# Reordering the tail of an attention and selected-row feed-forward kernel: row choice, picks, down projection and copies

## The chip, the cores and the metric

The kernel runs on one core of one Trainium2 chip. The metric is device microseconds of one execution. Where a ratio is quoted, it is the mean time of one kernel's fast runs over that of the other's fast runs of the same rounds, so not quite the ratio of the medians given beside it; in the experiments the first run of each kernel is left out of the ratio.

## The reference, cut to what matters

```python
def _A_ref(x, wq, wk, wv, wo):            # 16 query heads, one key/value head
    q = (x @ wq).reshape(B, S, 16, 28).transpose(0, 2, 1, 3)
    k, v = x @ wk, x @ wv
    p = softmax(einsum("bhqd,bkd->bhqk", q, k) * 28 ** -0.5)
    return heads_joined(einsum("bhqk,bkd->bhqd", p, v)) @ wo

def _B_ref(x, w_r, w_gate, w_up, w_down):  # 8 selected rows go through a feed-forward
    r = x @ w_r
    idx = argsort(-r)[:, :8]
    x_sel = x[idx]
    y = (silu(x_sel @ w_gate) * (x_sel @ w_up)) @ w_down
    return x + scatter_add(zeros, idx, y * sigmoid(r[idx]))

h  = x + _A_ref(layernorm(x), ...)         # x is 1 x 2048 x 448
h2 = h + _B_ref(layernorm(h), ...)         # gate/up 448 x 1792, down 1792 x 448
```

## The kernel before

The kernel handles 16 blocks of 128 rows. For each block TensorE forms scores, ScalarE takes most exponentials (VectorE and GpSimd make the rest with integer additions on the bit patterns, stored in Y), TensorE multiplies by the values, and the block's output is projected, added to x and normalized. When the last block is done, the eight rows with the largest router scores are found, gathered, sent through the feed-forward, and written over eight rows of the output. What follows the last exponential is called the tail here.

The program does not write its instructions in order. It declares operations with an assumed duration, what they read and write, and a priority; a planner puts them on the engines' queues. With `port=True` an operation is marked as one that VectorE is not to run beside GpSimd's marked work, and the planner starts it only when GpSimd's planned work with the mark is over:

```python
def dve_choice(self, lst, t, port):
    eff = [(max(o.ready, port) if o.port else o.ready, o) for o in lst]
    ...
```

GpSimd's large additions, its On products (attention output times reciprocal row sums), VectorE's On products of block 15 and others carry the mark. VectorE's On products of block 14 do not. A large addition reads:

```python
G.op(PO, lambda e: e.tensor_tensor(y[3].bitcast(I32), y[0].bitcast(I32),
                                   step3[:, 0:1].broadcast_to([128, 1024]), ALU.add), 2050, reads=r + ["step3"],
     writes=[("Y", n, 3, k) for k in range(4)], prio=t - 20, deps=done, port=True)
```

A check of the row sums reduces minima and maxima and adds the violation counts, one number per partition:

```python
spans = [(lall, lk, LO, HI, ())]          # blocks 0 to 14 together
if not exact:
    spans.append((Rb[:, rb, :], ..., (picked,)))
...
G.op(DV, lambda e: e.tensor_tensor(bad1[:, :], Lmm[:, 2:3], Lmm[:, 3:4], ALU.add), 70,
     reads=[("Ln", 0, 0), ("Ln", 0, 1)], writes=["bad1"])
for k in range(2 if not exact else 0):
    G.op(DV, lambda e, k=k: e.tensor_tensor(bad1[:, :], bad1[:, :], Lmm[:, 6 + k:7 + k], ALU.add), 70,
         reads=["bad1", ("Ln", 1, k)], writes=["bad1"])
```

The end of the kernel: VectorE copies the down projection's result and casts the output rows; then four row writes go out on SyncE's queue and four on ScalarE's. Each queue waits for all 16 ordinary output writes first, since a row write goes over what they wrote:

```python
for h, c in enumerate(halves):
    G.op(PE, mm(ps[0:8, obank[h], 0:224], pick8, part[:, c], False, True), 390, mode="F", ...)
    G.op(DV, lambda e, h=h, c=c: e.tensor_copy(rows8[:, c], ps[0:8, obank[h], 0:224]), 300, ...)
for j in range(8):
    q, ld = (SP, loads[0]) if j < 4 else (AC, loads[1])
    o = G.op(q, lambda e, j=j: e.dma_start(out[0, bass.ds(row[j], 1), :], rows8[j:j + 1, :]), 60,
             reads=[("rows8", 0), ("rows8", 1)] + [("out", k) for k in range(NT)], writes=[("scatter", j)], dma=True)
```

## Time and profile before

| Quantity | us |
|---|---|
| time, median of 3 runs | 389.06 |
| span in the profile | 386.9 |
| ScalarE idle ahead of its last five exponentials, at 361 | 0.76 |
| last exponential ends | 367.80 |
| output-row casts end | 383.29 |
| last exponential to end of casts | 15.49 |
| end of casts to end of span | 3.6 |

In the timeline each row has the start, the length, the engine, source line, operation and tiles, and in brackets the idle time before it with what ended it. Two rows of the timeline of before give the root of the 0.76 us: the residual addition of block 14 (hbuf) and the score matmuls that waited for it.

```profile
360.21 0.61 DVE L771 TENSOR_TENSOR hbuf<-ps,xx 128x448 f32<-128x448 f32 x1
...
360.96 0.40 PE L501 MATMUL ps<-Q,K 32*128 32x512 bf16 x4 [0.69 <-DVE hbuf L771]
```

### The profile page before, as it was taken

Reading aid. Unit: us, or ns where it says so; the run is one execution under the profiler, and the core shown is the slowest. Engines: PE = TensorE matmul, PEld = TensorE weight load, DVE = VectorE, ACT = ScalarE, POOL = GpSimd, SP = SyncE. Lnnn points to the kernel's source line nnn. Section 1 sums busy time; section 2 is a strip of 40 time slices with the busy share of each in tenths; the row PEclk is TensorE's granted clock in tenths of the full one; section 3 lists DMA queues with packets and bytes.
Section 4 is the critical chain, followed back from the end, with each engine's and each line's share of the span. In section 5 each row is a group of like instructions: output and inputs, shape, how many; then the busy total and the mean of one; then the engine's idle time right before and its main releaser. Section 6 shows DMA issues by size and latency. Waiting matters only on the chain.

```text
span 386.9 us, 8691 instructions
## 1 busy us (share of the span) xinstructions
PE 317.0 (82%) x3520; PEld 109.7 (28%) x3523; DVE 336.0 (87%) x706; ACT 365.2 (94%) x308; POOL 192.9 (50%) x185
## 2 busy tenths in 40 slices
PE   7899888878788887878788878878788888788895
PEld 3454332223223222323222222323232222222242
DVE  7996787989899897989798897979898998979973
ACT  4799999999999999999999999999999999999951
POOL 6520134645646375636546365746556464655410
PEclk9999999999999999999999999999999999999999
DMA  7995000010101010010102010010102010110100
GB/s 204 236 228 115 12 9 23 4 64 4 64 3 58 10 38 28 6 62 5 64 3 65 2 45 22 15 54 3 65 2 65 3 52 15 28 40 3 48 27 19
DMA packets 19557, 17.56 MB, mean 45 GB/s; under 512 B 5996, under 2 KB 16764, under 8 KB 19512
## 3 DMA queue, kind: packets, MB, share of 16 engines
q1 hardware_dynamic: 19472, 16.93, 16.2%
q8 instruction: 29, 0.48, 0.5%
q14 instruction: 16, 0.13, 0.1%
q0 software_dynamic: 32, 0.01, 0.0%
q10 hardware_dynamic: 8, 0.00, 0.0%
HBM read 11.43 MB, written 5.52 MB: 44 GB/s over the span
## 4 chain that ended last, share of the span: by engine, by line
ACT 81%; DVE 9%; PE 6%; DMA 1%; SPq 1%; issue 1%; POOL 0%; DVEq 0%
ACT P L928 81%; PE ps L501 5%; DVE bn L650 2%; DMA xx<-in_A_x_dram 1%; DVE Y L1005 1%; DVE xnT L694 1%; SPq L527 1%; DVE xx L679 1%; DVE K L711 1%; DVE mv L652 0%; POOL st L779 0%; DVE On L757 0%; DVE Y L1014 0%; PE ps L504 0%; DVE junk L807 0%
## 5 line engine op out<-in xcount | busy, mean ns | idle before, releaser
L928 ACT ACTIVATE P<-ps 128x1536 bf16<-128x1536 f32 (+1 forms) x281 | 354.2, 1510 | 3.4 <-PE ps L501 3.1
L1005 DVE TENSOR_SCALAR Y<-ps 128x512 int16<-128x512 f32 x240 | 164.9, 687 | 34.1 <-PE ps L501 34.1
L1021 POOL TENSOR_TENSOR Y<-Y,step 128x1024 int32<-128x1024 int32 x59 | 111.6, 1891 | 141.2 <-DVE Y L1014 140.6
L501 PE MATMUL ps<-Q,K 32*128 32x512 bf16 x1024 | 110.6, 382 | 60.7 <-DVE Y L1005 40.2
L501 PE MATMUL ps<-Y,Vs 128*32 128x512 bf16 x960 | 88.7, 384 | 1.6
L501 PEld LDWEIGHTS ps<-Q,K 32*128 32x128 bf16 x1024 | 33.1, 90 | 175.8 <-ACT P L928 168.4
L1014 DVE TENSOR_SCALAR Y<-Y 128x2048 int16<-128x2048 int16 x120 | 81.2, 687 | 0.6
L501 PE MATMUL ps<-P,Vs 128*32 128x512 bf16 x784 | 72.5, 385 | 0.0
L501 PE MATMUL ps<-zero 128*32 128x512 bf16 (+3 forms) x154 | 47.7, 383 | 1.6 <-DVE zero L520 1.2
L501 PEld LDWEIGHTS ps<-Y,Vs 128*32 128x32 bf16 x960 | 23.2, 94 | 31.7 <-issue 14.3
L501 PEld LDWEIGHTS ps<-P,Vs 128*32 128x32 bf16 x784 | 18.8, 94 | 28.1 <-issue 26.1
L754 POOL TENSOR_TENSOR On<-Ot,Rb 128x256 bf16<-128x256 f32 x28 | 19.7, 726 | 12.0 <-DMA Rb<-l_scr 12.0
L779 POOL TENSOR_TENSOR st<-st,nhalf 128x1 f32<-128x1 f32 x15 | 18.4, 1226 | 6.7 <-DVE st L777 6.7
L501 PEld LDWEIGHTS ps<-zero 128*32 128x32 bf16 (+1 forms) x157 | 13.5, 99 | 14.2 <-issue 6.8
L501 PE MATMUL ps<-xnT,wq_pad 112*128 112x128 bf16 x256 | 17.4, 220 | 0.0
L799 POOL TENSOR_SCALAR xx<-hbuf,st 128x448 bf16<-128x448 f32 x15 | 16.2, 1077 | 0.0
L501 PEld LDWEIGHTS ps<-xnT,wq_pad 112*128 112x128 bf16 x256 | 14.4, 98 | 3.6 <-issue 3.4
L501 PE MATMUL ps<-wo_pad,On 128*128 128x448 bf16 x64 | 14.9, 355 | 0.4 <-DVE On L757 0.4
L771 DVE TENSOR_TENSOR hbuf<-ps,xx 128x448 f32<-128x448 f32 x15 | 9.4, 623 | 2.3 <-PE ps L501 2.3
L637 DVE TENSOR_SCALAR Q<-ps,qone 128x512 bf16<-128x512 f32 x15 | 11.2, 749 | 0.0
L796 POOL TENSOR_SCALAR xx<-hbuf,st 128x448 bf16<-128x448 f32 x15 | 10.9, 726 | 0.5 <-DVE st L793 0.5
L650 DVE BATCH_NORM_STATS2 bn<-xx 128x6 f32<-128x448 bf16 x16 | 9.8, 613 | 1.2 <-DMA xx<-in_A_x_dram 1.1
(198 smaller groups left out, 172.5 us busy)
## 6 DMA issues: line engine op xcount, KB each, us to landing
Rb<-l_scr SPq DMA_DIRECT2D x14, 256.0 KB
x_scr<-xx SPq DMA_DIRECT2D x15, 224.0 KB, 2.4
out_dram<-xx SPq DMA_DIRECT2D x16, 112.0 KB, 1.7
wg_sb<-in_B_w_gate_dram SPq DMA_DIRECT2D x1, 1568.0 KB, 14.8
wu_sb<-in_B_w_up_dram SPq DMA_DIRECT2D x1, 1568.0 KB, 20.9
wd_sb<-in_B_w_down_dram SPq DMA_DIRECT2D x1, 1568.0 KB, 26.3
xx<-in_A_x_dram SPq DMA_DIRECT2D x3, 448.0 KB, 6.0
wq_sb<-in_A_wq_dram SPq DMA_DIRECT2D x2, 196.0 KB, 2.9
```

The source lines that it names most:

```text
L501: return lambda e: e.matmul(o, lhsT=l, rhs=r, start=start, stop=stop)
L637: G.op(DV, lambda e: e.tensor_scalar(Q[:, q, :, :].rearrange("p g n -> p (g n)"), ps[:, bank, :], qone[:, 0:1], None, ALU.add), dvt(512), ...
L650: G.op(DV, lambda e, t=t: e.bn_stats(bn6[:, t, :], x_sb[:, t, :]), dvt(D), reads=[("x", t)], writes=[("bn6", t)])
L754: G.op(PO, lambda e, c=c: e.tensor_tensor(On[:, rb, c], Ot[:, rb, c], Rb[:, rb, c], ALU.mult), 750, reads=[both[h], rk[h]], writes=[("On", ...
L771: G.op(DV, lambda e: e.tensor_tensor(hbuf[:, hr, :], ps[:, bank, 0:D], x_sb[:, t, :], ALU.add), dvt(D), reads=[pk(bank), ("x", t)], writes ...
L779: G.op(PO, lambda e: e.tensor_tensor(st[:, t, 4:5], st[:, t, 7:8], nhalf[:, 0:1], ALU.pow), 600, reads=[("st7", t), "nhalf"], writes=[("st ...
L796: G.op(PO, lambda e: e.tensor_scalar(outf[:, t, :], hbuf[:, hr, :], st[:, t, 5:6], st[:, t, 6:7], ALU.mult, ALU.add), 800, reads=[("h", hr ...
L799: G.op(PO, lambda e: e.tensor_scalar(xn[:, t, :], hbuf[:, hr, :], st[:, t, 4:5], st[:, t, 6:7], ALU.mult, ALU.add), 800, reads=[("h", hr), ...
L928: acts.append(G.op(AC, lambda e: e.activation(P[:, s0:s0 + w, :], ps[:, b0:b0 + w, :], ACT.Exp, bias=-(ZERO + SHIFT) * OCT, scale=OCT), w ...
L1005: G.op(DV, lambda e: e.tensor_scalar(Y[:, y, 0, q, :].bitcast(I16), ps[:, vb, :], 0.0, 32639.0 - STEP[3], ALU.max, ALU.min), dvt(512), rea ...
L1014: done = [G.op(DV, lambda e, c=c: e.tensor_single_scalar(y[c].bitcast(I16), y[0].bitcast(I16), STEP[c], ALU.add), 600, reads=r, writes=[(" ...
L1021: G.op(PO, lambda e: e.tensor_tensor(y[3].bitcast(I32), y[0].bitcast(I32), step3[:, 0:1].broadcast_to([128, 1024]), ALU.add), 2050, reads= ...
```

## The change

The intent is to shorten the chain of the tail, step by step, and to close the hole ahead of the last five exponentials. The core of the diff, with cuts marked:

```diff
-HINT = {PE: 118, AC: 8, DV: 8, PO: 1, SP: 6}
+HINT = {PE: 118, AC: 8, DV: 8, PO: 3, SP: 6}
...                                        (On products of the last blocks)
-                     reads=[both[h], rk[h]], writes=[("On", rb, h)], prio=G.prio - 500)
+                     reads=[both[h], rk[h]], writes=[("On", rb, h)], prio=G.prio - 500, urgent=not exact, port=True)
...                                        (GpSimd's large addition, third batch of block 15, is deferred)
+        if b == NB - 1 and j == 2:
+            done += [G.last_w[("On", b % 2 ^ 1, h)][-1] for h in range(2)] + [G.last_w[("st2", b - 2)][-1]]
...                                        (row choice alone; score broadcast later)
-        G.op(PE, [mm(ps[:, SB[1], 8:16], oneF[:, :], top8[:, :], True, True),
-                  mm(ps[0:8, SB[1], 24:25], eq8[0:NC1, :], cidx[:, :], True, True)], 400, mode="F", ...
+        G.op(PE, mm(ps[0:8, SB[1], 24:25], eq8[0:NC1, :], cidx[:, :], True, True), 200, mode="F", ..., prio=hot - 70)
...
+        G.op(PE, mm(ps[:, SB[1], 8:16], oneF[:, :], top8[:, :], True, True), 250, mode="F", ..., prio=hot + 9)
...                                        (picks: row numbers early, scores behind the up projection)
+    G.op(PE, [mm(ps[:, xbank, 0:1], rep4(128, 0), rsig[:, 1:2], True, False),
+              mm(ps[:, xbank, 0:1], rep4(8, 1), cols[:, 1:2], False, True)], 600, mode="F", deps=risen[-1:], ...
...                                        (down projection in two column halves, in two banks)
-            G.op(PE, [mm(ps[32 * c:32 * c + 32, dbank, 0:D], guT[0:CK, k, 32 * c:32 * c + 32], wd_sb[0:CK, 4 * c + k, :],
-                         k == 0, k == 3) for c in range(4)], 189, mode="V", ...
+        for n, x in enumerate(halves):
+            for k in (2 * h, 2 * h + 1):
+                down = G.op(PE, [mm(ps[32 * c:32 * c + 32, dbank[n], 0:224], guT[0:CK, k, 32 * c:32 * c + 32],
+                                    wd_sb[0:CK, 4 * c + k, x], k == 0, k == 3) for c in range(4)], 105, mode="V", ...
...                                        (copies and casts: one half on VectorE, one on ScalarE)
+    o = G.op(AC, lambda e: e.activation(part[:, halves[1]], ps[:, dbank[1], 0:224], ACT.Identity), 350, ...
...
+    G.op(DV, lambda e: e.tensor_copy(rows8[:, halves[0]], rest(0)), 300, ...
+    o = G.op(AC, lambda e: e.activation(rows8[:, halves[1]], rest(1), ACT.Identity), 350, ...
...                                        (row-sum check in three parts instead of two)
+        spans.append((Lc[:, NB - 2, :], [("Lc", NB - 2)], LO, HI, ()))
...
-    for k in range(2 if not exact else 0):
-        G.op(DV, lambda e, k=k: e.tensor_tensor(bad1[:, :], bad1[:, :], Lmm[:, 6 + k:7 + k], ALU.add), 70, ...
+    for n, k in ((n, k) for n in range(1, len(spans)) for k in range(2)):
+        G.op(DV, lambda e, n=n, k=k: e.tensor_tensor(bad1[:, :], bad1[:, :], Lmm[:, 4 * n + 2 + k:4 * n + 3 + k], ALU.add),
+             70, reads=["bad1", ("Ln", n, k)], writes=["bad1"])
```

More of the change, by code (lines that the diff above doesn't have):

```diff
@@ L428, in _main @@
     Rc = sb("Rc", [128, 2, 16], F32)
-    Lmm = sb("Lmm", [128, 8], F32)
+    Lmm = sb("Lmm", [128, 12], F32)
     Rb = sb("Rb", [128, 2, 512], F32)
@@ L493, in _main @@
     scr128 = junk[:, 0:128]
+    junk2 = xnT[:, 0, 0:896].bitcast(F32)
     R0, R1, VB, ACC = 5, 6, 6, 7
@@ L781, in out_proj @@
         if hurry:
-            G.op(DV, lambda e: e.scalar_tensor_tensor(junk[:, :], hbuf[:, hr, :], 1.0, w_rb[:, :], ALU.mult, ALU.mult,
+            G.op(DV, lambda e: e.scalar_tensor_tensor(junk2, hbuf[:, hr, :], 1.0, w_rb[:, :], ALU.mult, ALU.mult,
                                                       accum_out=st[:, t, 2:3]), 700,
-                 reads=[("h", hr), "w_rb"], writes=["junk", ("st2", t)], port=True, prio=G.prio - 890, urgent=True)
+                 reads=[("h", hr), "w_rb"], writes=[("xnT", k) for k in range(7)] + [("st2", t)], port=True, prio=G.prio - 890, urgent=True)
             G.op(DV, lambda e: e.tensor_scalar(st[:, t, 3:4], mv[:, t, 0:1], sw[:, 0:1], st[:, t, 2:3],
@@ L961, in sum_group @@
             o = G.op(PE, [None] * len(lst), 216, mode="V", pos=[x[0] for x in lst], reads=reads, deps=snap[1:] + first_sum,
-                     prio=G.prio - 0.005)
+                     prio=G.prio - 1.0)
             o.name = lst
@@ L1070, in stage2 @@
              reads=[pk(SB[1]), "pcol"], writes=["eq8"])
-        G.op(PE, [mm(ps[:, SB[1], 8:16], oneF[:, :], top8[:, :], True, True),
-                  mm(ps[0:8, SB[1], 24:25], eq8[0:NC1, :], cidx[:, :], True, True)], 400, mode="F",
-             reads=["cidx", "eq8", "oneF", "top8"], writes=[pk(SB[1])])
+        G.op(PE, mm(ps[0:8, SB[1], 24:25], eq8[0:NC1, :], cidx[:, :], True, True), 200, mode="F",
+             reads=["cidx", "eq8"], writes=[pk(SB[1])], prio=hot - 70)
         G.op(DV, lambda e: e.tensor_copy(cols[:, 0:1], ps[0:8, SB[1], 24:25]), 130, reads=[pk(SB[1])], writes=["cols0"])
         G.op(DV, lambda e: e.tensor_copy(idxu[:, :], cols[:, 0:1]), 70, reads=["cols0"], writes=["idxu"])
-        G.op(DV, lambda e: e.tensor_copy(bc[:, :], ps[:, SB[1], 8:16]), 130, reads=[pk(SB[1]), "cols0"], writes=["bc"], name="bc")
+        G.op(PE, mm(ps[:, SB[1], 8:16], oneF[:, :], top8[:, :], True, True), 250, mode="F", reads=["oneF", "top8"],
+             writes=[pk(SB[1])], prio=hot + 9)
+        G.op(DV, lambda e: e.tensor_copy(bc[:, :], ps[:, SB[1], 8:16]), 130, reads=[pk(SB[1])], writes=["bc"], name="bc",
+             prio=hot + 9)
     ot, sops, acts = [], [], []
@@ L1199, in _main @@
     G.prio = hot
-    rbank, xbank, gbank, ubank, tbank, kbank, dbank = 0, 1, 3, 6, 4, 4, 1
-    obank = (2, 6)
+    rbank, xbank, gbank, ubank, tbank, kbank, dbank = 0, 1, 3, 6, 4, 4, (1, 3)
+    obank = (2, 0)
     G.op(PE, mm(ps[:, rbank, 0:128], rp[:, t:t + 1].broadcast_to([128, 128]), ident[:, :], True, True), 60, mode="F",
@@ L1227, in _main @@
         for ch in range(NCH)]
-    wide(gbank, wg_sb, "wg_sb")
-    wide(ubank, wu_sb, "wu_sb")
+    halves = (slice(0, 224), slice(224, 448))
+    rest = lambda h: ps[32 * h:32 * h + 8, obank[h], 0:224]
+    for h, c in enumerate(halves):
+        G.op(PE, mm(rest(h), oh[0:8, 1, :], both8[:, c], True, False), 100, mode="F", reads=["oh1", "both8"],
+             writes=[pk(obank[h])], prio=hot + 1)
+    wide(gbank, wg_sb, "wg_sb")
+    risen = wide(ubank, wu_sb, "wu_sb")
+    G.prio = hot + 60
+    G.op(PO, lambda e: e.memset(junk[:, 128:384], 0.0), 300, reads=["junk"], writes=["ohf0", "ohf1"], prio=hot)
+    G.op(DV, lambda e: e.tensor_copy(ohf[:, 0, :, 0:8], oh[:, 0, :].unsqueeze(1).broadcast_to([128, 4, 8])), 90,
+         reads=["oh0"], writes=["ohf0"])
+    G.op(DV, lambda e: e.tensor_copy(ohf[0:8, 1, :, 0:8], oh[0:8, 1, :].unsqueeze(1).broadcast_to([8, 4, 8])), 90,
+         reads=["oh1"], writes=["ohf1"])
+    rep4 = lambda n, a: ohf[0:n, a, :, :].rearrange("p c n -> p (c n)")
+    G.op(PE, [mm(ps[0:1, kbank, 8:16], rsig[:, 0:1], ohf[:, 0, 0, 0:8], True, False),
+              mm(ps[0:1, kbank, 8:16], cols[:, 0:1], ohf[0:8, 1, 0, 0:8], False, True)], 200, mode="F",
+         reads=["ohf0", "ohf1", "rs0", "cols0"], writes=[pk(kbank)], prio=hot + 2)
+    G.op(DV, lambda e: e.tensor_copy(idx2, ps[0:1, kbank, 8:16]), 130, reads=[pk(kbank)], writes=["idx2"])
+    G.op(PE, [mm(ps[:, xbank, 0:1], rep4(128, 0), rsig[:, 1:2], True, False),
+              mm(ps[:, xbank, 0:1], rep4(8, 1), cols[:, 1:2], False, True)], 600, mode="F", deps=risen[-1:],
+         reads=["ohf0", "ohf1", "rs1", "cols1"], writes=[pk(xbank)])
+    G.op(DV, lambda e: e.tensor_scalar(pick8, mask8, ps[:, xbank, 0:1], None, ALU.mult), 90, reads=[pk(xbank), "mask8"],
+         writes=["pick8"])
+    G.prio = hot
     for h in range(2):
@@ L1250, in _main @@
     for h in range(2):
-        for k in (2 * h, 2 * h + 1):
-            G.op(PE, [mm(ps[32 * c:32 * c + 32, dbank, 0:D], guT[0:CK, k, 32 * c:32 * c + 32], wd_sb[0:CK, 4 * c + k, :],
-                         k == 0, k == 3) for c in range(4)], 189, mode="V", reads=[("guT", h), "wd_sb"],
-                 writes=[pk(dbank)])
-    halves = (slice(0, 224), slice(224, 448))
-    for h, c in enumerate(halves):
-        G.op(DV, lambda e, c=c: e.tensor_copy(part[:, c], ps[:, dbank, c]), 300, reads=[pk(dbank)],
-             writes=[("part", h)])
@@ L1259, in _main @@
-    G.prio = hot + 60
-    G.op(PO, lambda e: e.memset(junk[:, 128:384], 0.0), 300, reads=["junk"], writes=["ohf0", "ohf1"], prio=hot)
-    G.op(DV, lambda e: e.tensor_copy(ohf[:, 0, :, 0:8], oh[:, 0, :].unsqueeze(1).broadcast_to([128, 4, 8])), 90,
-         reads=["oh0"], writes=["ohf0"])
-    G.op(DV, lambda e: e.tensor_copy(ohf[0:8, 1, :, 0:8], oh[0:8, 1, :].unsqueeze(1).broadcast_to([8, 4, 8])), 90,
-         reads=["oh1"], writes=["ohf1"])
-    rep4 = lambda n, a: ohf[0:n, a, :, :].rearrange("p c n -> p (c n)")
@@ L1266, in _main @@
-    G.op(PE, [mm(ps[:, rbank, 0:1], rep4(128, 0), rsig[:, 1:2], True, False),
-              mm(ps[:, rbank, 0:1], rep4(8, 1), cols[:, 1:2], False, True),
-              mm(ps[0:1, rbank, 8:16], rsig[:, 0:1], ohf[:, 0, 0, 0:8], True, False),
-              mm(ps[0:1, rbank, 8:16], cols[:, 0:1], ohf[0:8, 1, 0, 0:8], False, True)], 600, mode="F",
-         reads=["ohf0", "ohf1", "rs0", "rs1", "cols0", "cols1"], writes=[pk(rbank)])
-    G.op(DV, lambda e: e.tensor_scalar(pick8, mask8, ps[:, rbank, 0:1], None, ALU.mult), 90, reads=[pk(rbank), "mask8"],
-         writes=["pick8"])
@@ L1273, in _main @@
-    G.op(DV, lambda e: e.tensor_copy(idx2, ps[0:1, rbank, 8:16]), 130, reads=[pk(rbank)], writes=["idx2"])
-    for h, c in enumerate(halves):
-        G.op(PE, [mm(ps[0:8, obank[h], 0:224], oh[:, 0, :], outf[:, t, c], True, False),
-                  mm(ps[0:8, obank[h], 0:224], oh[0:8, 1, :], both8[:, c], False, False)], 200, mode="F",
-             reads=["oh0", "oh1", ("outf", t), "both8"], writes=[pk(obank[h])])
+        for n, x in enumerate(halves):
+            for k in (2 * h, 2 * h + 1):
+                down = G.op(PE, [mm(ps[32 * c:32 * c + 32, dbank[n], 0:224], guT[0:CK, k, 32 * c:32 * c + 32],
+                                    wd_sb[0:CK, 4 * c + k, x], k == 0, k == 3) for c in range(4)], 105, mode="V",
+                            reads=[("guT", h), "wd_sb"], writes=[pk(dbank[n])])
@@ new lines, in _main @@
+    G.op(DV, lambda e: e.tensor_copy(part[:, halves[0]], ps[:, dbank[0], 0:224]), 300, reads=[pk(dbank[0])],
+         writes=[("part", 0)])
+    o = G.op(AC, lambda e: e.activation(part[:, halves[1]], ps[:, dbank[1], 0:224], ACT.Identity), 350,
+             reads=[pk(dbank[1])], writes=[("part", 1)])
+    o.deps[table.idx] = False
+    G.prio = hot + 60
+    for h, c in enumerate(halves):
+        G.op(PE, mm(rest(h), oh[:, 0, :], outf[:, t, c], False, False), 100, mode="F", reads=["oh0", ("outf", t)],
+             writes=[pk(obank[h])], deps=(down,), prio=hot - 1)
@@ L1288, in _main @@
     for h, c in enumerate(halves):
-        G.op(PE, mm(ps[0:8, obank[h], 0:224], pick8, part[:, c], False, True), 390, mode="F",
-             reads=["pick8", ("part", h), pk(obank[h])], writes=[pk(obank[h])])
-        G.op(DV, lambda e, h=h, c=c: e.tensor_copy(rows8[:, c], ps[0:8, obank[h], 0:224]), 300, reads=[pk(obank[h])],
-             writes=[("rows8", h)])
+        G.op(PE, mm(rest(h), pick8, part[:, c], False, True), 390, mode="F", reads=["pick8", ("part", h), pk(obank[h])],
+             writes=[pk(obank[h])])
+    G.op(DV, lambda e: e.tensor_copy(rows8[:, halves[0]], rest(0)), 300, reads=[pk(obank[0])], writes=[("rows8", 0)])
+    o = G.op(AC, lambda e: e.activation(rows8[:, halves[1]], rest(1), ACT.Identity), 350, reads=[pk(obank[1])],
+             writes=[("rows8", 1)])
+    o.deps[table.idx] = False
     done = []
@@ L1301, in _main @@
     G.prio = 7000
-    lall = Lc[:, 0:NB if exact else NB - 1, :].rearrange("p a b -> p (a b)")
-    lk = [("Lc", b) for b in range(NB if exact else NB - 1)]
+    nl = NB if exact else NB - 2
+    lall = Lc[:, 0:nl, :].rearrange("p a b -> p (a b)")
+    lk = [("Lc", b) for b in range(nl)]
     spans = [(lall, lk, LO, HI, ())]
@@ L1311, in _main @@
             G.op(DV, lambda e, m=m, k=k, src=src, red=red: e.tensor_reduce(m[:, k:k + 1], src, AX.X, red),
-                 dvt(512 if n else 256), reads=keys, writes=[("Lm", n, k)], deps=after)
+                 dvt((256, 16, 512)[n]), reads=keys, writes=[("Lm", n, k)], deps=after)
             G.op(DV, lambda e, m=m, k=k, cmp=cmp, lim=lim: e.tensor_single_scalar(m[:, 2 + k:3 + k], m[:, k:k + 1], lim,
@@ L1317, in _main @@
          reads=[("Ln", 0, 0), ("Ln", 0, 1)], writes=["bad1"])
-    for k in range(2 if not exact else 0):
-        G.op(DV, lambda e, k=k: e.tensor_tensor(bad1[:, :], bad1[:, :], Lmm[:, 6 + k:7 + k], ALU.add), 70,
-             reads=["bad1", ("Ln", 1, k)], writes=["bad1"])
-    G.op(PE, mm(ps[0:1, 0, 0:1], bad1[:, :], ones128[:, :], True, True), 100, mode="F", reads=["bad1", "ones128"],
-         writes=[pk(0)])
-    G.op(DV, lambda e: e.tensor_copy(flag[:, :], ps[0:1, 0, 0:1]), 120, reads=[pk(0)], writes=["flag"])
+    for n, k in ((n, k) for n in range(1, len(spans)) for k in range(2)):
+        G.op(DV, lambda e, n=n, k=k: e.tensor_tensor(bad1[:, :], bad1[:, :], Lmm[:, 4 * n + 2 + k:4 * n + 3 + k], ALU.add),
+             70, reads=["bad1", ("Ln", n, k)], writes=["bad1"])
+    G.op(PE, mm(ps[0:1, 6, 0:1], bad1[:, :], ones128[:, :], True, True), 100, mode="F", reads=["bad1", "ones128"],
+         writes=[pk(6)])
+    G.op(DV, lambda e: e.tensor_copy(flag[:, :], ps[0:1, 6, 0:1]), 120, reads=[pk(6)], writes=["flag"])
     G.op(DV, lambda e: e.tensor_copy(bad1[:, :], bad1[:, :]), 70, reads=["bad1", "flag"], writes=["bad1"])
```

## The prediction

> **What bounds the kernel now.** I read the shares of the page first, then the chain that ended last, then the timeline of the last 30 us, and there the stretches in which each engine stood still.
>
> From the page of the kernel before, the shares and the chain:
>
> ```profile
> PE 317.0 (82%) x3520; PEld 109.7 (28%) x3523; DVE 336.0 (87%) x706; ACT 365.2 (94%) x308; POOL 192.9 (50%) x185
> ...
> ACT 81%; DVE 9%; PE 6%; DMA 1%; SPq 1%; issue 1%; POOL 0%; DVEq 0%
> ```
>
> ScalarE's exponentials (281 instructions) are the bound for 81% of the chain, and the change does not touch them up to block 14 of 16. So most of the 386.9 us span cannot move. What can move lies after some 355 us: the last exponential ends at 367.80 (a run of five from 361.41, 6.39 long), and the span goes on for another 19.1 us. In the table by stages ScalarE has no work at all from 380.5 on, and TensorE does in sequence what VectorE hands it. There the bound is the length of a chain, not an engine.
>
> The ScalarE rows of the timeline from 359 to 361.5, and the TensorE rows from 369.9 to 374.1:
>
> ```profile
> 357.52 3.13 ACT L928 ACTIVATE P<-ps 128x1536 bf16<-128x1536 f32 x2
> 361.41 1.45 ACT L928 ACTIVATE P<-ps 128x1536 bf16<-128x1536 f32 x1 [0.76 <-PE ps L501]
> ```
>
> ```profile
> 370.42 0.38 PE L501 MATMUL ps<-top,oneF 1*128 1x8 f32 x2
> 370.73 0.20 PE L501 MATMUL ps<-cidx,eq 120*8 120x1 f32 x2
> 370.86 0.23 PE L501 MATMUL ps<-zero 128*128 128x128 bf16 x1
> 370.92 0.92 PE L501 MATMUL ps<-wo_pad,On 128*128 128x448 bf16 x4
> ```
>
> The first shows the one hole in ScalarE's late stream: 0.76 us at 361. The timeline names its root, since the score matmuls before it waited 0.69 us for the residual addition of block 14, which held their bank. The second shows the score broadcast (top) and the row choice (cidx, eq) ahead of the last output projection.
>
> The timeline around the selected rows:
>
> ```profile
> 375.23 0.34 PE L501 MATMUL ps<-wq_sb,xx 128*112 128x8 bf16 x4 [0.17 <-DVE wq_sb L1216]
> ...
> 375.43 0.43 PE L501 MATMUL ps<-zero 128*128 128x512 bf16 x2
> ...
> 375.79 0.36 PE L501 MATMUL ps<-wq_sb,Y 8*112 8x8 bf16 x4
> ...
> 376.09 0.38 PE L501 MATMUL ps<-rsig,junk 128*128 128x1 f32 x2
> 376.19 0.19 DVE L1223 CAST wq_sb<-ps 112x32 bf16<-112x32 f32 x1 [0.59 <-PE ps L501]
> ...
> 376.40 0.38 PE L501 MATMUL ps<-cols,junk 8*128 8x1 f32 x2
> ...
> 376.95 0.94 PE L501 MATMUL ps<-wg_sb,wq_sb 112*32 112x448 bf16 x16
> ```
>
> The selected rows are ready in VectorE's cast at 376.38, but the gate projection starts at 376.95: four float32 pick groups sit in front of it on TensorE's queue. And the rows fetched from memory had landed at about 374.8 (issue 372.31, 2.5 to landing), yet their matmul starts at 375.79, behind two filler matmuls.
>
> The end of the timeline, TensorE and VectorE:
>
> ```profile
> 380.48 0.94 PE L501 MATMUL ps<-wd_sb,Y 112*32 112x448 bf16 x16
> ...
> 381.47 0.69 DVE L1257 COPY Y<-ps 128x224 f32<-128x224 f32 x2 [1.13 <-PE ps L501]
> ...
> 381.95 0.92 PE L501 MATMUL ps<-Y,wq_sb 128*8 128x224 f32 x4
> ...
> 382.53 0.76 DVE L1291 CAST Y<-ps 8x224 bf16<-8x224 f32 x2 [0.37 <-PE ps L501]
> 383.44 1.63 ACTq L1296 DMA_DIRECT2D out_dram<-Y  x4
> ```
>
> From 380.48 to 383.44 each piece waits for the one before it.
>
> [...] The rows above have VectorE alone do the two copies of 0.34 and the two casts of 0.38. [...] the first On product of block 14 took 1.07 us while a GpSimd addition ran (355.55 to 357.44), the second, without it, 0.43.
>
> **The change part by part.** "Own estimate" holds for each end result.
>
> (a) Block 14. The GpSimd addition of the third batch of block 15 now waits until the On products and the score reduction of block 13 are done. On's first half then takes 0.43, not 1.07: 0.64 less. The check of the row sums is split, so that its 240-wide reductions (0.39 each, at 356.17 and 359.65) no longer wait for block 14 and can run in earlier slack; the second stood in front of the residual addition at 360.21. Together that addition comes about 1.0 earlier, more than the hole of 0.76 needs. I take 0.7 for ScalarE's end. The sums' matmuls ahead of the value matmuls might give 0.1 to 0.3 more in the logarithm and exponential; I count nothing for it. **-0.7.**
>
> (b) Row choice ahead of broadcast. Without the broadcast pair (0.38, about 0.31 of queue) and the filler, the first half of the last output projection can start when the first On product is done: 369.97 plus 0.37 is 370.34, plus 0.06 of semaphore is 370.4, where it started at 370.92. The second product ends at 370.71, which leaves its two matmuls to end at about 370.78 + 0.37 + 0.2 of drain = 371.35 instead of 371.84. **-0.4** of at most 0.5.
>
> (c) The index copies come about 0.4 earlier, and the fetch with them. Its data was no longer what the matmul waited for, but the kernel plans its own instruction order from assumed times, and two fillers (375.43 to 375.86) filled the expected wait. An earlier planned landing lets the matmul follow at about 375.5. **-0.3.**
>
> (d) Picks. Of the four groups (0.31 + 0.31 + 0.12 + 0.12 by their starts, 376.09 to 376.95) the two wide ones go behind the up projection. In their place may come the matmuls of the residual rows, 2 x 0.18 by the starts of such rows (379.95, 380.13, 380.32), partly in the wait for the cast. The gate then starts about 0.15 after the cast's end rather than 0.57. **-0.4.**
>
> (e) The wide picks behind the up projection take about 0.62 where residual matmuls, a flag and a filler stood (378.48 to 379.22, 0.74). The transposes need the first product, ready at 379.16. **+0.1** for a collision.
>
> (f) Down projection. Its first half needs the transposed block that ScalarE finished at 379.95; TensorE did residual matmuls (379.95 to 380.48) first. Half of these now come earlier and half after it. Start about 380.1. The second block arrives at 380.34, in time. Streaming stays 4 x 0.19 = 0.75 us, now 8 x 0.093; twice the weight loads (16 took 0.50 in union, under the streams) may add 0.1 to 0.2. Column half one is complete two groups, 0.2, before half two. **-0.25.**
>
> (g) Copies. Before, from the last down matmul (381.42) to the end of the casts (383.29): 1.87. Now VectorE copies half one 0.2 before the end and ScalarE half two beside it, so the picks are no longer kept behind the second copy; the float32 pick pairs still run in sequence, about 0.39 apart. Only one cast lies behind the last pick: 0.35 for 224 columns on ScalarE (0.30 of row spacing, 0.35 mean in the Silu rows) against the end of the second of two at 0.38. Worked from half one's end at -0.2: copy 0.05 + 0.34, pick 0.13 + 0.53, second pick 0.39 more, cast 0.05 + 0.35: 1.64. **-0.25.**
>
> (h) The ends of the row loads (0.51 and 0.50, at 377.4 and 380.0) precede the copy, so ScalarE's load does not delay it. The eight writes and their landing (383.44 to 386.9) stay: **0**.
>
> Sum: -0.7 - 0.4 - 0.3 - 0.4 + 0.1 - 0.25 - 0.25 = **-2.2**, so 389.06 becomes 386.86.
>
> **The rivals.** *A new order gives it back.* All instructions are ordered by the kernel's planner, so one moved operation shifts fillers and neighbours. The delayed GpSimd addition (1.89) now stands later, near the score reduction of block 14 and the power of 1.46, which bounded the snapshot at 365.30; if it collides there, (a) falls to nothing: 387.5. Against it, the power would have over 1 us of slack. *TensorE is the bound at the end of attention.* It is busy 6.34 of 7.0 us from 361 to 368, and fillers are in it. Then (a) yields 0.3: 387.2. *The halves lose.* If 32 short matmuls cost 0.3 more by their weights[...], (f) and (g) come to zero: 387.3. *Everything is hidden*: 389. Against it, the chain shows no parallel work behind which the tail could hide. For more: sums first and a better final order could bring 385.8.
>
> **Range and chances.** 386.8 us, with 8 in 10 between 385.6 and 388.2. Two per cent is 7.8 us, over a third of the whole 19.1 us tail plus the hole, and more than three times my sum. So: faster by over 2% 0.01, within 2% 0.985, slower 0.005.
>
> **What would show it.** ScalarE's gap of 0.76 gone and its last exponential near 367.1; On halves both near 0.43; the last projection about 0.4 after the first On product's start; gate within 0.3 of the cast; down projection starting right behind the second transposes; part copies overlapping on two engines; and the span some 2.2 shorter. I am wrong if the last exponential does not move, if the distance from it to the end stays at 19.1, or if down projection takes over 1.1.

Three figures can be found in the trace of before: the 0.06 "of semaphore" (block 14's second On product ends at 358.74, the weight load behind it starts at 358.80), the 0.2 "of drain" (a matmul of the last projection takes 0.35, and the next starts 0.19 behind it, so the last runs some 0.16 longer than the spacing) and ScalarE's 0.35 for 224 columns (the Silu rows, mean 354 ns). That ScalarE can copy one half beside VectorE was the author's estimate: no trace of before has it.

## More of the kernel before

When the queues are written out, a wait stands directly ahead of the first instruction on that queue that needs it:

```python
for o in self.orders[eng]:
    ...
    for s, v in w:
        e.wait_ge(s, v)
    ins = fn(e)
```

The view of one source line gives minimum, median and maximum of an instruction in ns. For ScalarE's four row writes of before it says:

```profile
L1296 ACTq DMA_DIRECT2D out_dram<-Y x4: 213/213/520, 383.4 to 384.9; - x4
```

The first takes 520 ns to issue and the others 213.

## The result and the profile after

| | before | after |
|---|---|---|
| time, median of 4 runs each, us | 388.94 | 391.63 |
| range, us | 388.58 to 389.76 | 391.14 to 391.71 |
| ratio of fast runs (95%) | | 1.0063 (1.0045 to 1.0082) |
| span in the profile, us | 386.9 | 389.3 |
| ScalarE's hole ahead of the last five exponentials | 0.76 | 1.65 |
| last exponential ends | 367.80 | 368.80 |
| last exponential to end of casts | 15.49 | 14.40 |
| end of casts to end of span | 3.6 | 6.1 |

The change is 2.7 us slower, within the 2% class but outside the predicted range and on the other side. The three parts of the span say where: the last exponential comes 1.0 later, the chain behind it is 1.1 shorter, and the row writes at the end take 2.5 longer. Their sum, +2.4, is the change of the span. In the page of after the chain still is ScalarE's, so no new engine has become the bound:

```profile
ACT 81%; DVE 8%; PE 7%; DMA 1%; SPq 1%; issue 1%
```

**The hole.** The timeline of after, all engines, around block 14's output:

```profile
356.58 0.72 POOL L800 TENSOR_SCALAR xx<-hbuf,st 128x448 bf16<-128x448 f32 x1
...
356.76 1.14 DVE L758 TENSOR_TENSOR On<-Ot,Rb 128x256 bf16<-128x256 f32 x2 [0.24 <-ACT Rb L750]
...
359.19 1.89 POOL L1024 TENSOR_TENSOR Y<-Y,step 128x1024 int32<-128x1024 int32 x1 [1.89 <-DVE Lmm L1331]
359.33 1.95 DVE L1337 TENSOR_TENSOR bad<-bad,Lmm 128x1 f32<-128x1 f32 x2
...
361.20 0.62 DVE L772 TENSOR_TENSOR hbuf<-ps,xx 128x448 f32<-128x448 f32 x1
...
361.97 0.40 PE L502 MATMUL ps<-Q,K 32*128 32x512 bf16 x4 [2.15 <-DVE hbuf L772]
...
362.41 2.79 ACT L929 ACTIVATE P<-ps 128x1536 bf16<-128x1536 f32 x2 [1.65 <-PE ps L502]
```

Read it downwards. The two On products now take 1.14 together, where before they took 1.07 and 0.43. That part worked by half. The large addition is out of their way, but the trace has the first product at 0.80 and the second at 0.41: the first now ran beside GpSimd's normalization (356.58 to 357.30) and ended 0.26 behind it, as it had ended 0.28 behind the large addition before. And the deferred addition now runs from 359.19 to 361.08, and in that time two VectorE additions of one number per partition take 1.95 us. By the view of that source line the longest took 1759 ns and the median 159. These are the check's additions. Before, the one of them at this place ran at 360.74 in 0.14 us, while GpSimd was idle. Behind them the residual addition starts at 361.20 instead of 360.21, the score matmuls wait 2.15 instead of 0.69, and ScalarE's hole is 1.65.

The table by stages of after has, behind the x-counted busy times of PE, PEld, DVE, ACT and POOL, the granted TensorE clock:

```profile
363.00:365.00 2.00, 2.00 (x26) 0.42 (x23) 2.00 (x8) 2.00 (x2) 1.14 (x1) 0.61 0.00 0
365.00:367.00 2.00, 2.00 (x23) 0.41 (x15) 1.50 (x6) 2.00 (x3) 0.86 (x2) 0.54 0.00 0
```

Before it was 1.00 in both. The stretch from 363.43 to 366.84, asked for alone, has 0.50 throughout. TensorE's gap of 2.15 us was followed by a slower clock; groups of four value matmuls took 0.61 to 0.64 instead of 0.39, and VectorE's copy of their result (Ot) waited 0.42 for TensorE.

**The tail.** The timeline of after, TensorE, VectorE and ScalarE, answers to the rows of before in the prediction:

```profile
372.00 0.92 PE L502 MATMUL ps<-wo_pad,On 128*128 128x448 bf16 x4
...
377.21 0.19 DVE L1228 CAST wq_sb<-ps 112x32 bf16<-112x32 f32 x1 [0.54 <-PE ps L502]
...
377.55 0.94 PE L502 MATMUL ps<-wg_sb,wq_sb 112*32 112x448 bf16 x16
...
380.86 0.95 PE L502 MATMUL ps<-wd_sb,Y 112*32 112x224 bf16 x32
...
381.67 0.39 DVE L1283 COPY Y<-ps 128x224 f32<-128x224 f32 x1 [0.67 <-PE ps L502]
...
381.86 0.36 ACT L1285 ACTIVATE Y<-ps 128x224 f32<-128x224 f32 x1 [1.31 <-PE ps L502]
...
382.85 0.35 ACT L1306 ACTIVATE Y<-ps 8x224 bf16<-8x224 f32 x1 [0.63 <-PE ps L502]
```

The gate projection follows the cast by 0.15 us instead of 0.57, the 32 half-width down matmuls take no longer than the 16 full ones (0.95 against 0.94), and the two copies overlap. All this is as intended.

**The end.** The view of the row writes' source line, after:

```profile
L1312 SPq DMA_DIRECT2D out_dram<-Y x4: 227/230/332, 383.4 to 384.8; - x4
...
L1312 ACTq DMA_DIRECT2D out_dram<-Y x4: 212/213/2784, 384.0 to 387.6; - x4
```

SyncE issues its four writes as before. ScalarE starts 0.5 us later, and its first write takes 2784 ns, where before it was 520. The records of ScalarE's queue show what stands before it, here the waits of before and then of after:

```profile
L362 ACTq EVENT_SEMAPHORE  x8: 38/38/38, 380.5 to 381.4; - x8
```

```profile
L362 ACTq EVENT_SEMAPHORE  x9: 17/38/38, 382.9 to 383.7; - x9
```

Before, eight instructions wait for the 16 ordinary output writes. ScalarE had no work there and ran them from 380.53 to 381.40, long before the rows were ready. Now ScalarE has the second cast, the waits (nine instructions, since one for the cast is among them) are written behind it because the row writes are what needs them, and they run from 382.86 to 383.79. In both kernels there is an extra pause of about 0.34 us among these waits, directly ahead of the 320th recorded instruction of this queue: it ends 2.3 us before the first write in before, 0.66 us in after. Packets of 8 KB follow it on one of the two DMA queues whose kind the page calls "instruction" (q14, with 16 packets and 0.13 MB in the whole run): at 381.36 and 381.79 in before, at 384.22 and 384.35 in after. No view says for which engine they are.

### The profile page after: what moved, and what is told of

Its sections match the earlier page's. It is cut to its first block, busy times and chain, and to the rows that moved or that the text cites. A ratio compares the mean times of both kernels' runs of the same rounds, so it can differ in the third digit from the quotient of the medians.

```text
span 389.3 us, 8720 instructions
## 1 busy us (share of the span) xinstructions
PE 316.4 (81%) x3530; PEld 109.9 (28%) x3533; DVE 335.5 (86%) x710; ACT 366.0 (94%) x310; POOL 192.7 (49%) x185
## 4 chain that ended last, share of the span: by engine, by line
ACT 81%; DVE 8%; PE 7%; DMA 1%; SPq 1%; issue 1%
ACT P L929 80%; PE ps L502 7%; DVE bn L651 2%; DMA xx<-in_A_x_dram 1%; DVE xnT L695 1%; SPq L528 1%; DVE Y L1006 1%; DVE xx L680 1%; DVE K L712 1%; DVE bad L1337 0%; DVE mv L653 0%; PE ps L505 0%; DVE On L758 0%; DVE var L674 0%; ACT xx L666 0%
## 5 line engine op out<-in xcount | busy, mean ns | idle before, releaser
L502 PE MATMUL ps<-Y,Vs 128*32 128x512 bf16 x960 | 89.6, 387 | 1.6
L502 PE MATMUL ps<-zero 128*32 128x512 bf16 (+3 forms) x148 | 46.5, 387 | 1.6 <-DVE zero L521 1.2
```

Source lines behind the costliest of these rows:

```text
L502: return lambda e: e.matmul(o, lhsT=l, rhs=r, start=start, stop=stop)
```

## The experiments

Two theories came from this.

- **A, collision:** the one-element additions are held by GpSimd's deferred addition, because the planner does not know that they collide with it. This makes the hole of 1.65 us and, as the theory has it, the slower clock behind it (0.50).
- **B, end of ScalarE's queue:** the slow first write costs some 2.5 us. B1: it comes from the place of the waits, and of the pause of 0.34 us among them, which now stand directly ahead of the write. B2: it is the hint for the final branch, which is placed by counting instructions from the queue's end and runs at 378.55 in after, where before it ran at 374.19.

Rivals: the change's own steps cost the time (32 half-width matmuls, ScalarE's copies), or the deferral itself is at fault (it lets GpSimd start late).

The experiments ran on three chips: one for the first four told below, a noisy one for the next four but the repeat of both mends, and a third for that repeat and the last two. Each group shares its runs of before, whose medians were 389.19, 390.02 and 388.65 us. From the recorded expectations clauses are cut that told what no trace shows; where they name B1, it is the theory as put above.

### Marking the additions (only A is mended)

```diff
-             70, reads=["bad1", ("Ln", n, k)], writes=["bad1"])
+             70, reads=["bad1", ("Ln", n, k)], writes=["bad1"], port=True)
```

> The changed kernel with one edit: the two extra one-element additions of the row-sum check are declared to use the port [...], so the planner puts them after the GpSimd addition (1.89 us) instead of beside it. Theory A (one of them was held 1.76 us by that addition, and kept the residual addition of block 14, the score matmuls and ScalarE waiting; TensorE then stood 2.15 us and lost its clock): the residual addition starts near 359.6 instead of 361.2, ScalarE's hole of 1.65 us falls under 0.4, the granted clock stays 1.00 from 363 to 367, the last exponential ends near 367.2 instead of 368.8, and the time falls by 1.3 to 2.0 us against the changed kernel. Rival (the residual addition waits for something else, such as the output projection or a later place of the port): the hole stays over 1 us and the time falls by under 0.5.

Measured: 388.65 us (388.21 to 389.47) against 389.19 of before, ratio 0.9974 (0.994 to 1.0009). The timeline, ScalarE and VectorE, and the additions' source line:

```profile
357.10 10.83 ACT L929 ACTIVATE P<-ps 128x1536 bf16<-128x1536 f32 x8
...
360.32 0.62 DVE L772 TENSOR_TENSOR hbuf<-ps,xx 128x448 f32<-128x448 f32 x1
```

```profile
L1337 DVE TENSOR_TENSOR bad<-bad,Lmm x4: 149/155/243, 365.3 to 377.8; 128x1 f32<-128x1 f32 x4
```

The last eight exponentials run through without a hole; the first two additions have moved to 365. By the traces the order of all other instructions on TensorE, VectorE, ScalarE and GpSimd is that of after, so the mark did nothing else. This execution has the row of exponentials 0.8 us later than after (0.4 of it already at the first exponential, 10.97 instead of 10.54), so positions are compared with the row of exponentials beside them: the residual addition starts 3.22 us behind its start at 357.10, where in after it is 4.90 (361.20 less 356.30) and in before 4.02 (360.21 less 356.19). The clock is 1.00 in every window from 359 to 367. Against the repeat of after on the same chip (390.95, below) the gain is 2.3 us: the hole of that repeat's profile, 1.87 and 0.16, is 2.0 of it, and the rest is within the scatter of the runs. The first row write still took 2471 ns. The collision and the hole are shown, and the gain is larger than I expected. The clock's part in it is less certain (see "What stays open").

### Waits paid early (only B is mended)

```diff
-    loads = [G.op(..., reads=["idx2"], writes=[("row", j0)], name="load", ...
+    loads = [G.op(..., reads=["idx2"] + [("out", k) for k in range(NT)], writes=[("row", j0)], name="load", ...
```

The load of the row numbers into registers precedes ScalarE's copies on its queue. If it waits for the 16 output writes, the row writes no longer have to.

> The changed kernel with one edit: the row-number loads also wait for the sixteen output writes, so those waits stand before the loads and not between ScalarE's last cast and its four row writes. Theory B1 (the first row write of ScalarE's queue took 2.78 us [...] since the waits were moved behind the cast): its first write starts within 0.3 us of SyncE's and takes 0.5 us, and the time falls by 2.2 to 2.9 against the changed kernel. Rival B2 (the branch hint, executed 5.4 us before the first write instead of 9.2, makes it slow): the write still takes about 2.8, and only the 0.5 of the waits is won.

Measured: 389.27 us (388.93 to 389.85), ratio to before 0.9999 (0.9964 to 1.0034); 1.7 below the repeat of after. The row writes:

```profile
L1312 ACTq DMA_DIRECT2D out_dram<-Y x4: 212/213/519, 383.6 to 385.0; - x4
```

From the end of the casts to the end of the span it is 3.72 us instead of 6.1. The pause among the waits now ends at 381.04, 2.5 us before the first write. The hole of 1.65 and the clock's fall (0.50 from 363 to 365) are still there. B1 holds for the position of the waits: by the trace nothing on the four compute engines is ordered otherwise than in after. It also rules out that the cast directly ahead makes the write slow, since the cast still stands there (383.03 to 383.38). The timed gain of 1.7 is less than the 2.4 of the profiles; the slow write varied between kernels without this mend (2784, 2655, 2471, 2032 and 2003 ns).

### The hint elsewhere (rival B2)

```diff
-HINT = {PE: 118, AC: 8, DV: 8, PO: 3, SP: 6}
+HINT = {PE: 118, AC: 10, DV: 8, PO: 3, SP: 6}
```

> The changed kernel with one edit: ScalarE's branch hint two instructions earlier, so it executes near 375 as in the kernel before. Rival B2 (the late hint makes the first row write slow): the write falls from 2.78 us to about 0.5 and the time by about 2.3. Theory B1 [...]: no change, within 0.3 us of the changed kernel.

Measured: 391.03 us (390.37 to 392.65), ratio 1.0053 (1.0011 to 1.0095). The hint ran at 375.21, far from the writes, and the first write still took 2003 ns. B2 falls.

### Twelve empty instructions at the start (failed as an experiment)

```diff
-    G.op(AC, lambda e: e.preload_act_table_set("natural_log_exp_and_others"), 1400)
+    G.op(AC, [lambda e: e.preload_act_table_set("natural_log_exp_and_others")] + [lambda e: e.nop()] * 12, 1400)
```

> The changed kernel with one edit: twelve empty instructions at the start of ScalarE's queue, where it has time, so that everything behind stands twelve places later [...]. Theory B1: the pause of 0.38 us among the waits goes, the first row write takes about 0.5 instead of 2.78, ScalarE's writes still start some 0.2 to 0.5 after SyncE's because of the waits, and the time falls by about 2.3 to 2.6. Rival B2 (hint) or B3 (ScalarE's own cast just before makes the write slow): no change within 0.3.

The build left the empty instructions out: the trace has the same 342 ScalarE instructions as that of after. So it tested nothing of B1, but it is a repeat of after on the same chip as the runs above: 390.95 us (390.6 to 392.46), ratio 1.0045 (1.0003 to 1.0086), first write 2655 ns.

### Twenty-four satisfied waits early in ScalarE's queue

```diff
             elif o.sig:
                 ins.then_inc(self.sems[eng], 1)
+            if eng == AC and not self.after and o is self.orders[AC][60]:
+                for _ in range(24):
+                    e.wait_ge(self.sems[PE], 1)
```

These make 12 instructions that wait for nothing, so everything behind them moves by 12 places.

> The twelve empty instructions of the fourth run are not in its trace (the build dropped them), so it repeated the changed kernel. Here the shift is made with twelve instructions that wait for a semaphore value long reached, put into ScalarE's queue early among the exponentials[...]. Theory B1 [...]: the pause of about 0.38 us moves twelve instructions earlier, before the Silu, and the first write falls from 2 to 2.8 us to about 0.5; its start stays some 0.4 us behind SyncE's, since the waits stay; the time falls by 1.8 to 2.4 against the changed kernel. Rival B4 (the waits themselves, or ScalarE's cast right before, make the write slow): it still takes over 1.8 and the time stays within 0.4.

Measured: 391.6 us (391.05 to 392.3), ratio to before 1.0017 (0.9949 to 1.0084); this chip was noisy, with the clock of before between 0.986 and 1.000. The row writes:

```profile
L1315 ACTq DMA_DIRECT2D out_dram<-Y x4: 212/213/519, 384.7 to 386.1; - x4
```

The pause has left the waits and the first write is back at 519 ns with the waits still late, so the pause's place, not the waits themselves, decides. But the end did not get shorter: from the casts' end to the span's end it is still 6.0 us, where after has 6.1. ScalarE's final branch now took from 386.99 to 389.95, with packets on the queue q14 starting at 387.84 to 387.93; in before the same step took 0.49. So what the first write no longer takes, the branch now does; no view names why. Shifting is therefore no mend; with the one that works, the pause ended 2.5 us before the first write.

### Both mends

The two edits of the first two experiments together.

> Both mends together on the changed kernel: the two one-element additions behind the GpSimd addition, and the output waits ahead of the row-number loads. If the two costs are independent and add up, 391.6 minus 2.6 (first run) minus 2.2 (second run) gives 386.5 to 387.2, some 0.5 to 0.7% under the kernel before. If one hides the other, it stays above 388.

Measured: 386.55 us (386.2 to 387.09) against 390.02 on the noisy chip, ratio 0.9893 (0.9827 to 0.9959). ScalarE's timeline:

```profile
356.07 10.83 ACT L929 ACTIVATE P<-ps 128x1536 bf16<-128x1536 f32 x8
```

There is no hole, the last exponential ends at 366.90, the casts 13.92 us behind it, the span 3.7 behind these, and the first row write took 519 ns.

> The kernel with both mends again, on the same chip as the two runs before, so that they can be compared: 386.2 to 387.2 us where before has 389.0, ratio 0.991 to 0.995, no hole before the last eight exponentials and a first output-row write of about 520 ns on ScalarE's queue.

Measured on the quieter chip: 386.49 us (386.31 to 387.17) against 388.65, ratio 0.9945 (0.9919 to 0.9972), with 13.94 and 3.73 for the two distances. Each mend moves its own part of the span and leaves the other's (1.65 or no hole, 5.8 or 3.7 at the end), so the two causes are separate and add up. This version beats both kernels.

### One cast on ScalarE in the kernel before (B alone, from the other side)

```diff
 for h, c in enumerate(halves):
     ...
-        G.op(DV, lambda e, h=h, c=c: e.tensor_copy(rows8[:, c], ps[0:8, obank[h], 0:224]), 300, ...
+        if h:
+            o = G.op(AC, lambda e, c=c: e.activation(rows8[:, c], ps[0:8, obank[1], 0:224], ACT.Identity), 350, ...
+            o.deps[table.idx] = False
+        else:
+            G.op(DV, lambda e, h=h, c=c: e.tensor_copy(rows8[:, c], ps[0:8, obank[h], 0:224]), 300, ...
```

> The kernel before with one part of the change alone: the cast of the second half of the output rows on ScalarE instead of VectorE, nothing else. By itself it should save nothing (0.35 against 0.38 us). Theory B1 with the waits: the sixteen output waits now stand behind that cast, [...] the first write of ScalarE's queue starts about 0.4 us late and takes 2 to 2.8 us; the time rises by 2.0 to 2.8 over the kernel before. Rival (the loss needs the other parts of the change): within 0.4 of the kernel before.

Measured: 391.94 us (390.73 to 392.94) against 390.02, ratio 1.0018 (0.9948 to 1.0087). The ratio decides nothing: the clock fell in this profile too (0.72 and 0.50 from 363 to 367, without the change's collision: TensorE's gaps from 357 to 363 were 0.67, 0.69 and 0.57, as in the profile of before), and it varied in before. The profile does decide. The timeline and the row writes:

```profile
384.64 0.35 ACT L1292 ACTIVATE Y<-ps 8x224 bf16<-8x224 f32 x1 [2.76 <-PE ps L501]
```

```profile
L1301 ACTq DMA_DIRECT2D out_dram<-Y x4: 213/213/2757, 385.7 to 389.4; - x4
```

From the casts' end to the span's end it is 6.0 us instead of 3.6. A single cast moved to ScalarE, with nothing else of the change, brings the whole cost of B.

### Without the deferral (rival to A)

```diff
-        if b == NB - 1 and j == 2:
-            done += [G.last_w[("On", b % 2 ^ 1, h)][-1] for h in range(2)] + [G.last_w[("st2", b - 2)][-1]]
```

> The changed kernel without the rule that makes the GpSimd addition of block 15 wait for the products and the score reduction of block 14. Theory A: the addition runs from about 355.7 again, the first product takes about 1.07 us as in the kernel before, the one-element additions are not held, ScalarE's hole is 0.3 to 0.9 us instead of 1.65, the clock stays at 1.00 from 363 to 367, the end of the kernel stays slow; time down by 0.8 to 1.6 against the changed kernel. Rival: no change, so the deferral is not what made the additions collide.

Measured: 389.62 us (389.35 to 390.17) against 390.02, ratio 0.9973 (0.9907 to 1.0039). The timeline of GpSimd and VectorE:

```profile
355.63 1.89 POOL L1022 TENSOR_TENSOR Y<-Y,step 128x1024 int32<-128x1024 int32 x1 [0.90 <-DVE Y L1015]
...
356.63 1.14 DVE L1335 TENSOR_TENSOR bad<-bad,Lmm 128x1 f32<-128x1 f32 x2
```

Without the deferral the addition runs at its old time, and the check's additions, moved forward with the split, meet it there: the longest took 907 ns and ended as GpSimd's did. The On products came behind them, at 358.29 instead of 356.76 in after, and the hole is 0.94. The expectation had them not held, and was wrong there. So the deferral alone is not at fault: the unmarked additions run into GpSimd's work in either place, only at the later one there is more left of it to wait for. This run is less clean than the others, since the planner also moved other work (five more matmuls).

### No dummy matmuls, and fewer, in the tail

The planner fills TensorE's gaps with matmuls on zeros. These two runs ask, as theory F, why moving the row choice and the gathered rows gave little, both on top of the two mends. In the first the tail has no dummies, in the second only where the recent load falls under 0.6.

```diff
         if late and not self.todo[b]:
+            return None
```

```diff
         if late and not self.todo[b]:
             ...
-            if self.recent(s) >= self.FLOOR0:      # 0.85
+            if self.recent(s) >= 0.6:
```

> The kernel with both mends (the one-element additions marked as users of the port [...], and the output-write waits paid early), and in the tail no dummy matmuls between real ones. Theory F (steps b and c of the prediction moved nothing because dummy matmuls planned into TensorE's gaps still stand ahead of the row choice, of the last projection and of the gathered rows' matmul): from the last exponential's end the first selected-row matmul comes at 7.1 or earlier instead of 7.5, the gathered rows' matmul within 0.2 us of it instead of 0.5, and the time is 0.3 to 0.8 us below the kernel with both mends. Rival (the dummy matmuls keep the granted clock up): the clock after the last exponential falls under 0.9 and the time is the same or up to 2 us longer. Rival (the matmuls after them wait for data, so that the dummies lie in idle time): same time within 0.2 us, same distances.

> As the run before, but the dummy matmuls of the tail are only planned where the recent load falls under 0.6 instead of 0.85. Theory F: between the kernel with both mends and the one without dummies, 0.1 to 0.5 us below the former. Rival of the clock: as the run before if the floor of 0.85 matters, else the same time as the kernel with both mends.

Measured, against 388.65 of before and 386.49 of both mends: 387.96 us (387.54 to 389.17) without dummies, ratio 0.9975 (0.9949 to 1.0), and 387.64 us (386.51 to 387.85) with fewer, ratio 0.9972 (0.9947 to 0.9997). The first's table by stages:

```profile
370.00:375.00 5.00, 2.31 (x20) 1.56 (x18) 3.92 (x22) 3.24 (x6) 1.51 (x2) 0.87 0.02 5
375.00:380.00 5.00, 4.94 (x44) 2.68 (x42) 2.70 (x11) 0.96 (x3) 0.00 (x0) 0.50 0.08 26
```

Without dummies the row choice started 2.07 us behind the last exponential instead of 2.46, and the first selected-row matmul 0.27 earlier (6.75 against 7.02, by 373.64 less 366.89 and 373.95 less 366.93). So dummies did stand in the way, by 0.3 to 0.4. But the clock fell to 0.50 for the rest of the tail, where with both mends and the dummies it is 1.00 (370 to 380), the gate projection took 1.69 instead of 0.94, and the distance to the casts' end grew from 13.9 to 16.7. (This profile is of the slowest of the four runs; by the medians the loss is 1.5.) With fewer dummies the one execution at a clock of 1.000 took 386.51; the other three, at 0.993 to 0.995, took 387.48 to 387.85. Here the dummies are worth more than they cost (386.49 us with them by the medians, 387.96 without). The rival, that they keep the clock up, was right: 1.00 with them, 0.50 without.

## Why the prediction went wrong, step by step

| Step | Predicted, us | After, measured | With both mends |
|---|---|---|---|
| (a) block 14 and ScalarE's hole | -0.7 | +1.0 | -0.9 |
| (b) row choice to last projection | -0.4 | +0.1 | -0.4 |
| (c) gathered rows | -0.3 | -0.06 | -0.02 to -0.05 |
| (d) picks | -0.4 | -0.42 | -0.42 |
| (e), (f) collision, start of down projection | -0.15 | -0.22 | -0.22 |
| (g) copies | -0.25 | -0.48 | -0.47 |
| (h) row writes | 0 | +2.5 | +0.1 |
| sum | -2.2 | +2.4 | -2.3 to -2.4 |

The measured values are differences of distances in the profiles (the last exponential's end for (a), from it to the last projection's start for (b), then from stage to stage), so they add up to the change of span, apart from some 0.05 in between. Position (a) contains the noise of the loads at the start of an execution, a few tenths. That the sum with both mends comes so near to the predicted one is in part luck: (c) gave some 0.26 less than predicted and (g) 0.22 more.

**(a) failed.** The prediction said that the 240-wide reductions would "run in earlier slack", and reckoned the GpSimd addition's new place only against two operations, the score reduction and the power. It did so although it had seen that the first On product took 1.07 us beside GpSimd's addition and the second 0.43 without it, and had counted 0.64 us from that. It did not ask which other VectorE instructions stand near 359, and did not mention the one-element additions at all. The first rival, that a new order gives it back, was right in kind, but it named other operations and put a bottom of 0 under the loss. The runs showed 1.65 instead of 0.76, by an addition that does almost nothing and waited 1.6 us. A smaller miss is On's first half: it was to take 0.43, "0.64 less", and took 0.80, since GpSimd's normalization moved into the addition's place. With the mark set the residual addition comes 0.80 earlier than in before (3.22 instead of 4.02, predicted was about 1.0), and the hole is gone, as predicted.

**(b) was mis-sized in its own step and lost by (a).** The projection was to start some 0.4 behind the first On product's start; it started 0.77 behind it (372.00 less 371.23), and 0.76 to 0.77 with both mends, since three dummies (four with both mends) and the row choice stayed in front of it. From the end of the last of the three small matmuls ahead of the row choice (oneF, trow) to the projection it went from 1.19 to 0.93 in after, and the same with both mends. But in after the selection before it came later by 0.34, since VectorE's copy waited 0.42 for value matmuls at the slower clock (0.50). With the clock at 1.00 the whole of (b) is -0.4, but only 0.26 of it comes from this step; the other 0.15 is an earlier selection, which (b) did not name, so that the number agrees by luck. The dummies that stayed in front of the row choice cost 0.3 to 0.4 more, but without them the clock fell to 0.50.

**(c) was mis-sized.** The matmul of the gathered rows follows the first selected-row matmul by 0.50 instead of 0.56, since one dummy of 512 columns stayed in front of it. Without dummies it is 0.38, at the price just told.

**(d), (e) and (f) were right.** The gate follows the cast by 0.15. From gate to down projection it went from 3.53 to 3.31. The half-width down projection is as long as the full-width one (0.95 and 0.94); the "0.1 to 0.2" for its weight loads didn't come.

**(g) was right and too small.** From the end of the down matmuls to the end of the casts it went from 1.87 to 1.39. With a bank for each half the first copy starts before the second half's matmuls are done (381.67 against 381.81), and the four pick matmuls take 0.70 instead of 0.92.

**(h) failed, by the larger part.** "The eight writes and their landing", it said, stay at 0; they took 2.5 more. That looked at the load of row numbers and at landing times, not at what else ScalarE's queue holds: the 16 waits, which the idle time that ends with the change had hidden. Step (g) filled that idle time with two copies. The prediction saw "ScalarE has no work at all from 380.5 on" in the table by stages and took it for an engine that was free; its queue was not.

Both failed steps have the same shape: work that the busy times do not show (a held addition of 0.15 us, waits of no busy time at all) had been harmless by position, and the change moved it.

What stays open: what the slow write waits for was not shown. It goes with the pause's place: 2784 ns where the pause ends 0.66 us ahead of the write, 519 or 520 where it ends 2.3 or 2.5 us ahead or is moved out of the waits by 12 instructions. No view names the reason of the 2.8 us. Nor is it shown what makes the clock fall. It fell to 0.50 in all five profiles in which ScalarE's hole was 1.65 to 1.87 us (after, waits early, hint, empty instructions, satisfied waits) and in none of those with the additions marked, up to the last exponential; but it fell to 0.50 in the one-cast run too, whose gaps were those of before. In the experiments' runs of before, 18 of 21 executions have a mean clock under 1.000 (0.986 to 0.998, on all three chips), so the profile of before, with 1.000, is not its usual execution. The eight executions with both mends have 0.997 to 1.000, so a part of their lead over before may be the clock.

## What to carry to other kernels

Before giving an idle engine new work in a tail, read its queue and not only its busy time: waits and register loads take time on it too, and here they lay in that idle time (in before a register load of 0.50 us and the waits from 380.53 to 381.40, with the pause of 0.34 among them); when new work filled it, the first write took 2784 ns instead of 520. Mark every instruction of the kind that a trace shows held by another engine, however small: the wait here had the length of what was left of the other engine's instruction (1.6 us) and not of its own (0.15). When a change of several steps comes out slower though most of them gain, split the span at two or three fixed points (here the last exponential and the end of the casts) before anything else; the steps that gained and the places that lost separate at once.
